# Attention and a feed-forward layer on one core: value tiles 144 instead of 132 bytes apart, attention outputs 288 instead of 264 bytes apart in PSUM

## The chip, the cores and the metric

One of the cores of a Trainium2 chip runs the whole program. The metric is the device time of one execution in microseconds, taken over several executions. The granted TensorE clock was 1.000 in all profiles shown below. Two words for the memories: SBUF holds what TensorE reads, PSUM the fp32 sums that it writes.

## The reference

Grouped-query attention (8 batches, 16 query heads, 4 key/value heads, 384 positions, head size 64), then a feed-forward layer with squared ReLU (1024 to 2048 to 1024), over 3072 tokens:

```python
scores = (1 / sqrt(64)) * q @ k.T          # k, v repeated for 4 query heads each
attn   = exp(scores - max) / sum
x      = (attn @ v) as [3072, 1024]
out    = (relu(x @ w_in) ** 2) @ w_out
```

## The kernel before

The kernel computes the scores transposed, so the exponentials can serve directly as the stationary operand (the one that is loaded first, by a weight load) of the second attention matmul. Its moving operand (the one that is streamed through, column by column) is a value tile of 128 positions by 64 values, with a column of ones behind them: output column 64 is then the softmax denominator. Each output needs three accumulating matmuls (j = 0, 1, 2), six outputs (f) share one PSUM bank, and VectorE divides them on the way out. A scheduler that runs on the host decides the order of all instructions from fixed costs, which do not depend on any address.

```python
DP = D + 2                                            # D = 64
v_aug = [sb(f"v_aug{i}", [128, NU, DP]) for i in range(2)]      # NU = 12 value tiles of a batch, bf16
...
R.add(eng, lambda e: e.tensor_copy(v_aug[b % 2][:, :, 0:D], v_st[b % NST][:, :, :]), ...)   # on GpSimd (POOL)
...
def av(b, c, banks):                                  # half a head group: 18 matmuls
    g, s2 = c // 2, c % 2
    i = pick(banks)
    po = bank(i)[:, 0:2 * NJ * DP].rearrange("p (f e) -> p f e", f=2 * NJ)      # fp32, PSUM

    def mm(pe, f0):
        for f in range(f0, f0 + NJ):                  # NJ = 3
            for j in range(NJ):
                w = expT[:, (b * NU + g * NJ + j) % NEX, f % 2, (f // 2) * 128:(f // 2) * 128 + 128]
                m = pe.matmul(po[:, f - 6 * s2, 0:D + 1], w, v_aug[b % 2][:, g * NJ + j, 0:D + 1],   # L383
                              start=(j == 0), stop=(j == NJ - 1))
        return m
    ...
    R.add("vector", lambda e: e.reciprocal(rinv[r].ap().unsqueeze(2), po[:, :, D:D + 1]), ...)
    ...
    srcv = po[:, :, 0:D].rearrange("p (s i) d -> p s i d", s=2)
    R.add("vector", lambda e: e.tensor_tensor(dst, srcv, rbv, ALU.mult), ...)
...
R.add("vector", lambda e, i=i: e.memset(v_aug[i][:, :, D:D + 1], 1.0), writes=[("v_one", i)])
# cuts: loads, transposes, scores (L358), exp (L368), up-projection (L440), down-projection (L496), scheduler
```

The softmax here doesn't subtract the row's maximum and nothing guards it: scores larger than these inputs give would overflow.

## Time and profile before

| | before |
|---|---|
| time, median of 3 runs | 427.7 us (427.55 to 427.76) |
| span of the profiled run | 426.2 us |
| TensorE busy | 420.4 us, 99% |
| matmuls of L383 | 1152, of 65 columns |

First the page of the kernel before: the span, the busy time of each engine, the chain of waits that ended last (share of the span by engine, then by line), and the groups that the change touches. A group's columns are line, engine, operation, output and inputs, shape and count; then busy us and mean ns of one; then idle time of the engine before it.

```profile
span 426.2 us, 7813 instructions
...
PE 420.4 (99%) x3435; PEld 232.0 (54%) x3464; DVE 157.9 (37%) x332; ACT 194.8 (46%) x194; POOL 55.4 (13%) x68
...
PE 96%; DMA 1%; issue 1%; ACT 1%; POOL 1%; DVE 0%; POOLq 0%
PE ps L440 40%; PE ps L496 39%; PE ps L383 8%; PE ps L358 7%; DMA q_st<-in_q_dram 1%; PE ps L337 1%; ACT expT L347 1%; PE ps L311 0%; PE ps L416 0%; POOL q_st L239 0%; PE ps L294 0%; POOL v_st L232 0%; DVE qT L318 0%; DVE y_sb L505 0%; POOL
...
L383 PEld LDWEIGHTS ps<-v_aug,expT 128*128 128x128 bf16 x1152 | 40.0, 97 | 6.9 <-issue 0.6
L383 PE MATMUL ps<-v_aug,expT 128*128 128x65 bf16 x1152 | 42.0, 193 | 0.0
L398 DVE TENSOR_TENSOR o_sb<-ps,rinv 128x384 bf16<-128x384 f32 x64 | 35.7, 558 | 2.2
...
L392 DVE RECIPROCAL rinv<-ps 128x6 f32<-128x6 f32 x64 | 12.2, 190 | 27.3 <-PE ps L383 27.3
```

TensorE is the bound: 96% of the chain, the feed-forward lines L440 and L496 taking four fifths of it, L383 8%. The 193 ns of one L383 matmul is a latency with much overlap; 42.0 us over 1152 matmuls is already only 36 ns each. The useful number is the time from one start to the next (a step; the expectations call a slow one a slip).

The chain in order of time (start us, us, what), two of its L383 runs with what follows each:

```profile
...
144.06 1.12 PE ps L383 x36
145.18 1.30 PE ps L440 x8
...
147.23 3.35 PE ps L440 x20
150.59 1.12 PE ps L383 x36
```

A full run of 36 matmuls takes 1.12 us, 31 ns per matmul, with no gap before or after it. And the view of line L383 (minimum, median and maximum duration in ns, then the start of the first and of the last in us):

```profile
...
L383 PE MATMUL ps<-v_aug,expT x1152: 191/193/205, 10.9 to 293.9; 128*128 128x65 bf16 x192
```

From the first L383 matmul to the last 283.0 us pass (10.9 to 293.9). Where the order of instructions is the same, this stretch compares kernels without their start-up, which differs between runs by some tenths of a us. It still contains every wait of TensorE on the way, so it is checked below against the steps themselves.

### The profile page before, as it was taken

To read this page: it belongs to the slowest core of one execution; us is meant where nothing else is said; L and a number is where in the kernel's file an instruction comes from. 1 tells how busy PE (TensorE), PEld (TensorE's weight loads), DVE (VectorE), ACT (ScalarE), POOL (GpSimd) and SP (SyncE) were. 2 spreads that over 40 slices of the span, in tenths; PEclk is the share of its full clock that TensorE was granted. 3 is DMA by queue.
4 is the path that set the end of the run, shared out by engine and by line. 5 is a ranking of instruction groups with operands and counts; after the bars stand their busy time and mean duration, and the time that the engine had idled before them with its cause. 6 is when DMAs were issued, how large, how long until landed. Compare 5 with 4: busy or idle time off the path is not lost.

```text
span 426.2 us, 7813 instructions
## 1 busy us (share of the span) xinstructions
PE 420.4 (99%) x3435; PEld 232.0 (54%) x3464; DVE 157.9 (37%) x332; ACT 194.8 (46%) x194; POOL 55.4 (13%) x68
## 2 busy tenths in 40 slices
PE   8999999999999999999999999999999999999997
PEld 6565554555545555455554455544564465446544
DVE  3664431343424443144442344422441244114412
ACT  6957730477355773547745377552240033003300
POOL 8680001234013004003100000000000000000000
DMA  9999999999789178938918321033001100110012
GB/s 177 184 184 200 186 201 226 180 158 158 145 182 167 26 106 125 149 94 134 120 45 180 92 34 25 12 88 102 25 2 49 74 26 2 49 74 26 1 67 82
DMA packets 96915, 44.30 MB, mean 104 GB/s; under 512 B 77296, under 2 KB 90864, under 8 KB 96880
## 3 DMA queue, kind: packets, MB, share of 16 engines
q0 software_dynamic: 36544, 17.44, 32.1%
q1 hardware_dynamic: 59664, 25.86, 28.7%
q8 instruction: 27, 0.44, 0.4%
q10 hardware_dynamic: 672, 0.49, 0.4%
q14 instruction: 8, 0.07, 0.1%
HBM read 35.65 MB, written 12.58 MB: 113 GB/s over the span
## 4 chain that ended last, share of the span: by engine, by line
PE 96%; DMA 1%; issue 1%; ACT 1%; POOL 1%; DVE 0%; POOLq 0%
PE ps L440 40%; PE ps L496 39%; PE ps L383 8%; PE ps L358 7%; DMA q_st<-in_q_dram 1%; PE ps L337 1%; ACT expT L347 1%; PE ps L311 0%; PE ps L416 0%; POOL q_st L239 0%; PE ps L294 0%; POOL v_st L232 0%; DVE qT L318 0%; DVE y_sb L505 0%; POOL ident L523 0%
## 5 line engine op out<-in xcount | busy, mean ns | idle before, releaser
L440 PE MATMUL ps<-xT,w_in_sb 128*128 128x384 bf16 x1024 | 174.8, 326 | 0.0
L496 PE MATMUL ps<-w_out_sb,h2T 128*128 128x512 bf16 (+2 forms) x755 | 167.5, 375 | 1.9 <-issue 0.5
L368 ACT ACTIVATE expT<-ps 128x3072 bf16<-128x3072 f32 x42 | 114.5, 2727 | 64.8 <-PE ps L358 64.0
L440 PEld LDWEIGHTS ps<-xT,w_in_sb 128*128 128x128 bf16 x1024 | 97.0, 98 | 69.6 <-issue 6.8
L450 ACT ACTIVATE h2T<-hr 128x384 bf16<-128x384 f32 x128 | 64.5, 520 | 140.9 <-DVE hr L448 140.9
L496 PEld LDWEIGHTS ps<-w_out_sb,h2T 128*128 128x128 bf16 x784 | 73.8, 98 | 87.1 <-issue 5.1
L448 DVE TENSOR_SCALAR hr<-ps 128x384 f32<-128x384 f32 x128 | 71.2, 557 | 106.4 <-PE ps L440 106.4
L505 DVE COPY y_sb<-ps 128x512 f32<-128x512 f32 (+2 forms) x49 | 33.4, 681 | 122.8 <-PE ps L496 122.8
L383 PEld LDWEIGHTS ps<-v_aug,expT 128*128 128x128 bf16 x1152 | 40.0, 97 | 6.9 <-issue 0.6
L383 PE MATMUL ps<-v_aug,expT 128*128 128x65 bf16 x1152 | 42.0, 193 | 0.0
L398 DVE TENSOR_TENSOR o_sb<-ps,rinv 128x384 bf16<-128x384 f32 x64 | 35.7, 558 | 2.2
L358 PE MATMUL ps<-qT,kT 64*128 64x512 bf16 (+1 forms) x336 | 34.6, 325 | 0.0
L358 PEld LDWEIGHTS ps<-qT,kT 64*128 64x128 bf16 x336 | 13.0, 94 | 20.7 <-issue 6.3
L392 DVE RECIPROCAL rinv<-ps 128x6 f32<-128x6 f32 x64 | 12.2, 190 | 27.3 <-PE ps L383 27.3
L271 POOL COPY v_aug<-v_st 128x768 bf16<-128x768 bf16 x8 | 6.6, 831 | 83.9 <-PE ps L383 68.4
L347 ACT ACTIVATE expT<-ps 128x1024 bf16<-128x1024 f32 (+1 forms) x20 | 16.9, 980 | 1.1 <-PE ps L337 0.8
L266 POOL COPY k_dup<-k_st 128x1536 bf16<-128x1536 bf16 x7 | 10.3, 1470 | 43.5 <-DMA k_st<-in_k_dram 43.5
L239 POOL DMA_DIRECT2D q_st<-in_q_dram x17 | 14.8, 883 | 0.9 <-POOLq L751 0.8
L207 POOL DMA_DIRECT2D k_st<-in_k_dram x7 | 5.3, 757 | 39.4 <-DMA qT<-q_st 39.4
L337 PE MATMUL ps<-qT,kT 64*128 64x384 bf16 (+2 forms) x48 | 7.5, 343 | 0.3 <-ACT expT L347 0.2
L249 POOL DMA_DIRECT2D w_in_sb<-in_moe_w_in_dram x8 | 7.1, 891 | 0.0
L232 POOL DMA_DIRECT2D v_st<-in_v_dram x8 | 6.3, 784 | 0.1
(26 smaller groups left out, 41.9 us busy)
## 6 DMA issues: line engine op xcount, KB each, us to landing
out_dram<-y_sb SPq DMA_DIRECT2D x47, 256.0 KB, 2.0
q_st<-in_q_dram POOLq DMA_DIRECT2D x14, 384.0 KB, 8.2
w_in_sb<-in_moe_w_in_dram POOLq DMA_DIRECT2D x8, 512.0 KB, 14.5
w_out_sb<-in_moe_w_out_dram POOLq DMA_DIRECT2D x4, 1024.0 KB, 30.8
v_st<-in_v_dram POOLq DMA_DIRECT2D x8, 192.0 KB, 9.8
k_st<-in_k_dram POOLq DMA_DIRECT2D x7, 192.0 KB, 4.4
q_st<-in_q_dram POOLq DMA_DIRECT2D x3, 192.0 KB, 5.4
xT<-o_sb SPq DMA_TRANSPOSE x28, 3.1
```

What stands on the lines that cost most here:

```text
L239: R.add("gpsimd", lambda g: g.dma_start(q_st[st][:, h0:h1, :], q[b, h0:h1].rearrange("h (p j) d -> p h (j d)", j=NJ)), writes=[("q_st", st ...
L347: R.add("scalar", lambda e: e.activation(dst, src, AF.Exp, scale=0.125), reads=keys, writes=[("expT", (b * NU + u) % NEX, t) for u, _, _ i ...
L358: m = pe.matmul(flat[:, k0 * HC + c0:k0 * HC + c1], kT[b % 2][64 * x:64 * x + 64, u + k0, :], q_cols(b, (u + k0) // NJ, x, c0, c1))
L368: R.add("scalar", lambda e: e.activation(dst, src, AF.Exp, scale=0.125), reads=keys, writes=[("expT", (n + m) % NEX, t) for m in range(2) ...
L383: m = pe.matmul(po[:, f - 6 * s2, 0:D + 1], w, v_aug[b % 2][:, g * NJ + j, 0:D + 1], start=(j == 0), stop=(j == NJ - 1))
L392: R.add("vector", lambda e: e.reciprocal(rinv[r].ap().unsqueeze(2), po[:, :, D:D + 1]), reads=[("bank", i)], writes=[("rinv", r)], cost=0.13)
L398: R.add("vector", lambda e: e.tensor_tensor(dst, srcv, rbv, ALU.mult), reads=[("bank", i), ("rinv", r)], writes=[("o_sb", o, s2)], cost=0.48)
L440: m = pe.matmul(bank(i)[:, 0:S], w_in_sb[:, kc, c * 128:(c + 1) * 128], xT[b % NXT][:, kc, :], start=(kc == 0), stop=(kc == NKC - 1))
L448: R.add("vector", lambda e: e.tensor_scalar_max(hr[r][:, :], bank(i)[:, 0:S], 0.0), reads=[("bank", i)], writes=[("hr", r)], cost=0.48)
L450: R.add("scalar", lambda e: e.activation(h2T[b % 2][:, c, :], hr[r][:, :], AF.Square), reads=[("hr", r)], writes=[("h2T", b % 2, c)], cost ...
L496: m = pe.matmul(bank(i)[:, 0:n], h2T[b % 2][:, c, i3 * 128:(i3 + 1) * 128], w_out_sb[:, c, c0:c1], start=(c == 0), stop=(c == NFC - 1))
L505: R.add("vector", lambda e: e.tensor_copy(ysl, bank(i)[:, 0:n]), reads=[("bank", i)], writes=[("y", yb)], cost=0.08 + n / 960)
```

## The change

The intent: 132 bytes is no multiple of 16, so the value tiles start at all four residues 0, 4, 8 and 12 modulo 16. At 144 = 9 x 16 bytes, all start on a multiple of 16. The PSUM outputs follow the same constant and go from 66 to 72 fp32 words apart.

```diff
-    DP = D + 2
+    DP, DV = D + 8, D + 8
...
-    v_aug = [sb(f"v_aug{i}", [128, NU, DP]) for i in range(2)]
+    v_aug = [sb(f"v_aug{i}", [128, NU, DV]) for i in range(2)]
```

## The prediction

> **What bounds the kernel.** TensorE. The page shows PE busy 99% of a 426.2 us span; the chain of waits that ended last is 96% PE, with clock 1.000. By line, that chain spends 40% on the up-projection (L440), 39% on the down-projection (L496), 8.3% on the attention-times-value matmuls (L383, the only ones the change touches) and 7% on scores.
>
> **What the change does.** Same instructions, same order, same shapes. Only addresses move: the 12 value tiles of one batch go from 132 to 144 bytes apart in SBUF (they are the moving operand, 65 bf16 columns read), and the six outputs of one PSUM bank from 264 to 288 bytes apart. Later SBUF buffers shift by 288 bytes, a multiple of 32.
>
> **Cost now.** L383 has 1152 matmuls; the chain shows a full run of 36 as 1.10 to 1.13 us. Taking start-to-start times of consecutive L383 matmuls from the trace (batches 1 to 7), the mean is 31.1 ns. Sorted by value tile n, so by start (132n mod 16):
>
> - start at 0 (n = 0, 4, 8): 29.2, 29.2, 29.2 ns, spread 0.4
> - start at 4 (n = 1, 5, 9): 33.1, 33.5, 29.2
> - start at 8 (n = 2, 6, 10): 32.2, 31.2, 32.9
> - start at 12 (n = 3, 7, 11): 29.5, 32.8, 31.9
>
> Tiles that start on a multiple of 16 bytes always run at 29.2; most others cost 2 to 4 ns more. The Trainium skill, "Advanced Engine Details and Errata", section Memory Cachelines, gives SBUF lines of 16 bytes; the trace agrees with a penalty of that period. The skill's "TensorE: Matmul & The Clock Gate", section "Wait — 56ns, not 53.3ns?", gives start-to-start of N / 2.4 GHz plus about 2.5 ns, 29.6 ns for N = 65: the aligned tiles are already there (29.2), so the floor is stream length.
>
> **Gain.** With 144 = 9 x 16 bytes every tile starts on a line. Estimate: (31.1 - 29.2) ns x 1152 = 2.2 us; batch 0 (31.8 ns) may give slightly more. All L383 blocks sit inside the unbroken PE chain, so nearly all of it should show.
>
> **PSUM half.** 264 and 288 are both multiples of 8, and the aligned tiles show 29.2 with spread 0.4 over all six output slots, so I give it nothing. The reciprocal (190 ns) and the normalizing multiply (557 ns) read runs of the same length and should not move.
>
> **Predicted time:** 425.5 us, 80% range 424.5 to 427.0. Faster by over 2%: 1%. Within 2%: 98%. Slower by over 2%: 1%.
>
> **What would show it.** L383 blocks of 36 fall from about 1.12 to about 1.05 to 1.06 us; start-to-start about 29.3 ns for every n, with no dependence on n; PE busy total down by about 2 us; L440 (163 ns apart), L496 (216 ns) and all DVE and ACT durations unchanged. If instead times still depend on n, the line theory is wrong; if all L383 get about 30.5, weight loads hold the rate and the gain is below 1 us.
>
> **What would make it wrong.** Weight loads (also 31 ns apart) may have their own limit that the slow tiles now hide. The saving could turn into waits for DVE, ACT or, in the first 60 us, weight DMAs. Shifted buffers (xT, w_in, w_out) might suffer from an address effect I cannot see, on 78% of the chain; a 1% change there would outweigh the gain.

## The result, and the profile after

| | before | after |
|---|---|---|
| time, median of 6 runs each | 427.87 us (427.55 to 428.86) | 427.52 us (427.21 to 428.14) |
| ratio, 95% interval | | 0.9991 (0.9977 to 1.0004) |
| span of the profiled run | 426.2 us | 425.4 us |
| TensorE busy | 420.4 us | 419.9 us |
| first to last L383 start | 283.0 us | 282.3 us |
| L383 start to start, mean | 31.13 ns | 30.45 ns |

A ratio is the mean time of one kernel's runs over that of the other's of the same rounds, so not quite the ratio of the medians quoted. Executions over 1.5% slower than the fastest of the same kernel are left out of the means. The median lies outside the predicted range (424.5 to 427.0): the gain is about a third of the 2.2 us forecast. The clock time alone cannot tell it from nothing, but the trace can.

The same parts of the page of the kernel after:

```profile
span 425.4 us, 7813 instructions
...
PE 419.9 (99%) x3435; PEld 231.6 (54%) x3464; DVE 157.8 (37%) x332; ACT 194.9 (46%) x194; POOL 55.3 (13%) x68
...
PE 96%; DMA 1%; issue 1%; ACT 1%; POOL 1%; DVE 0%; POOLq 0%
PE ps L440 40%; PE ps L496 39%; PE ps L383 8%; PE ps L358 7%; DMA q_st<-in_q_dram 1%; PE ps L337 1%; ACT expT L347 1%; PE ps L311 0%; PE ps L416 0%; PE ps L294 0%; POOL q_st L239 0%; POOL v_st L232 0%; DVE qT L318 0%; DVE y_sb L505 0%; POOL
...
L383 PEld LDWEIGHTS ps<-v_aug,expT 128*128 128x128 bf16 x1152 | 39.2, 97 | 6.9 <-issue 0.6
L383 PE MATMUL ps<-v_aug,expT 128*128 128x65 bf16 x1152 | 41.2, 193 | 0.0
L398 DVE TENSOR_TENSOR o_sb<-ps,rinv 128x384 bf16<-128x384 f32 x64 | 35.7, 557 | 2.2
...
L392 DVE RECIPROCAL rinv<-ps 128x6 f32<-128x6 f32 x64 | 12.2, 190 | 27.0 <-PE ps L383 27.0
```

Only L383 moved: 0.8 us less busy time, for its matmuls and for its weight loads (whose starts keep the same distance to those of the matmuls in both traces). VectorE's times are what they were. The order of instructions is the same on every engine. The chain in order of time and the view of L383, after:

```profile
...
143.70 1.09 PE ps L383 x36
144.79 1.30 PE ps L440 x8
...
146.85 3.36 PE ps L440 x20
150.21 1.09 PE ps L383 x36
```

```profile
...
L383 PE MATMUL ps<-v_aug,expT x1152: 191/193/204, 10.8 to 293.1; 128*128 128x65 bf16 x192
```

A run of 36 takes 1.09 us instead of 1.12; 1.05 to 1.06 was predicted. From the first L383 to the last it is 282.3 us (10.8 to 293.1), 0.7 less. Nothing took the gain back: in the list of waits, the scores (L358) wait for VectorE and for exp exactly as long as before:

```profile
...
PEld ps L358 <- DVE o_sb L398: 4.2, 13, 0.4
...
PEld ps L358 <- ACT expT L368: 2.0, 6, 0.4
```

```profile
...
PEld ps L358 <- DVE o_sb L398: 4.2, 13, 0.4
...
PEld ps L358 <- ACT expT L368: 2.0, 6, 0.4
```

The first fence is of before, the second of after; the columns are who waited for whom: us in total, times, longest us. Start to start, the up-projection runs at 162.8 ns in both traces and the down-projection (512 columns) at 216.0, leaving out ten double steps in each trace where a record is missing. So the missing 1.4 us was never gained at L383 itself.

Start-to-start times in ns of one run of 36 (batch 3, first key/value group), worked out from the start times in the two traces, show what happened:

```
before  29 35 32 30 32 33 29 33 33 29 32 33 29 32 32 29 34 32 29 33 32 29 34 32 29 34 32 29 33 32 30 32 32 29 33
after   29 35 30 29 29 35 29 29 29 35 30 29 29 29 35 29 29 30 29 35 29 29 29 29 35 30 29 29 35 29 29 29 30 35 29
```

The values of 32 to 34 that came with the mixed starts are gone, and the dependence on the tile n with them (batches 1 to 7, means for every n: 30.1 to 31.2). But every fourth or fifth step is now 35 ns, for tiles that all start on a multiple of 16 bytes (aligned, below), which the kernel before shows at 29.2 only. 29 ns is a step that happens, not a rate that lasts.

### The profile page after: what moved, and what is told of

Same layout as the page of the kernel before. It is cut to its first block, busy times and chain, and to the rows that moved or that the text cites. A ratio compares the mean times of both kernels' runs of the same rounds, so it can differ in the third digit from the quotient of the medians.

```text
span 425.4 us, 7813 instructions
## 1 busy us (share of the span) xinstructions
PE 419.9 (99%) x3435; PEld 231.6 (54%) x3464; DVE 157.8 (37%) x332; ACT 194.9 (46%) x194; POOL 55.3 (13%) x68
## 4 chain that ended last, share of the span: by engine, by line
PE 96%; DMA 1%; issue 1%; ACT 1%; POOL 1%; DVE 0%; POOLq 0%
PE ps L440 40%; PE ps L496 39%; PE ps L383 8%; PE ps L358 7%; DMA q_st<-in_q_dram 1%; PE ps L337 1%; ACT expT L347 1%; PE ps L311 0%; PE ps L416 0%; PE ps L294 0%; POOL q_st L239 0%; POOL v_st L232 0%; DVE qT L318 0%; DVE y_sb L505 0%; POOL ident L523 0%
## 5 line engine op out<-in xcount | busy, mean ns | idle before, releaser
L440 PE MATMUL ps<-xT,w_in_sb 128*128 128x384 bf16 x1024 | 174.8, 326 | 0.0
L496 PE MATMUL ps<-w_out_sb,h2T 128*128 128x512 bf16 (+2 forms) x755 | 167.5, 375 | 1.9 <-issue 0.5
L440 PEld LDWEIGHTS ps<-xT,w_in_sb 128*128 128x128 bf16 x1024 | 97.0, 98 | 69.5 <-issue 6.8
L496 PEld LDWEIGHTS ps<-w_out_sb,h2T 128*128 128x128 bf16 x784 | 73.8, 98 | 87.0 <-issue 5.1
L383 PEld LDWEIGHTS ps<-v_aug,expT 128*128 128x128 bf16 x1152 | 39.2, 97 | 6.9 <-issue 0.6
L383 PE MATMUL ps<-v_aug,expT 128*128 128x65 bf16 x1152 | 41.2, 193 | 0.0
L358 PE MATMUL ps<-qT,kT 64*128 64x512 bf16 (+1 forms) x336 | 34.6, 325 | 0.0
L358 PEld LDWEIGHTS ps<-qT,kT 64*128 64x128 bf16 x336 | 13.0, 94 | 20.7 <-issue 6.3
## 6 DMA issues: line engine op xcount, KB each, us to landing
w_out_sb<-in_moe_w_out_dram POOLq DMA_DIRECT2D x4, 1024.0 KB, 31.1
```

What stands on the lines that cost most here:

```text
L358: m = pe.matmul(flat[:, k0 * HC + c0:k0 * HC + c1], kT[b % 2][64 * x:64 * x + 64, u + k0, :], q_cols(b, (u + k0) // NJ, x, c0, c1))
L440: m = pe.matmul(bank(i)[:, 0:S], w_in_sb[:, kc, c * 128:(c + 1) * 128], xT[b % NXT][:, kc, :], start=(kc == 0), stop=(kc == NKC - 1))
L496: m = pe.matmul(bank(i)[:, 0:n], h2T[b % 2][:, c, i3 * 128:(i3 + 1) * 128], w_out_sb[:, c, c0:c1], start=(c == 0), stop=(c == NFC - 1))
```

## The experiments

All numbers called the mean are start to start between neighbouring L383 matmuls in batches 1 to 7, without the last of each run. Each comes from one trace; the pairs that differ only in the PSUM spacing (before and psum_only, after and sbuf_only) or in the element that is read (cols64 and bcast64) agree to 0.01 ns. The L383 records are complete (1152) in every trace; other lines lack a few, so totals of other lines are not compared. Edits are against the kernel after. "Wrong" means that the results do not match the reference and need not. The medians of the kernel before, in the rounds that were timed, lie between 427.9 and 428.0 us. The columns with numbers of bytes say where in a 16-byte line of SBUF the read starts, and how far apart the outputs lie in PSUM ("+ 4": each starts 4 bytes later).

| run | columns | start in a 16-byte line | PSUM | mean, ns | steps of 34 ns or more | checked result |
|---|---|---|---|---|---|---|
| before | 65 | 0, 4, 8, 12 mixed | 264 | 31.13 | 8% | right |
| after | 65 | 0 | 288 | 30.45 | 22% | right |
| sbuf_only | 65 | 0 | 264 | 30.46 | 22% | right |
| psum_only | 65 | mixed | 288 | 31.14 | 9% | right |
| cols64 | 64 | 0 | 288 | 29.14 | 0% | wrong |
| cols32 | 32 | 0 | 288 | 25.28 | 0% | wrong |
| cols66 | 66 | 0 | 288 | 30.44 | 22% | right |
| cols72 | 72 | 0 | 288 | 32.43 | 0% | right |
| ones_first | 65 | 14 | 288 + 28 | 30.88 | 34% | right |
| sbuf80 | 65 | 0 (160 apart) | 288 | 30.53 | 23% | right |
| sbuf68 | 65 | 0, 8 mixed | 288 | 30.64 | 17% | right |
| cols68 | 68 | 0 | 288 | 31.14 | 17% | right |
| cols64_132 | 64 | 0, 4, 8, 12 mixed | 264 | 29.98 | 5% | wrong |
| cols57 | 57 | 0 | 288 | 26.71 | 0% | wrong |
| bcast65 | 65 (one element repeated) | | 288 | 29.95 | 0% | wrong |
| bcast64 | 64 (one element repeated) | | 288 | 29.14 | 0% | wrong |
| cols64_psum4 | 64 | 0 | 288 + 4 | 29.96 | 0% | wrong |
| cols64_off8 | 64 | 8 | 288 | 29.21 | 0% | wrong |
| cols65_off8 | 65 | 8 | 288 | 30.02 | 9% | right |
| cols64_off4 | 64 | 4 | 288 | 29.21 | 3% | wrong |

### Which half of the change acts: sbuf_only and psum_only

```diff
-    DP, DV = D + 8, D + 8
+    DP, DV = D + 2, D + 8      # sbuf_only
+    DP, DV = D + 8, D + 2      # psum_only
```

> Value tiles 144 bytes apart, outputs still 264. Theory: the SBUF half does everything, so start-to-start of the L383 matmuls has the after kernel's pattern (29 ns with slips of 35 ns about every fifth, mean 30.4 to 30.5 ns in batches 1 to 7, no dependence on tile n) and the time is that of after (ratio to before 0.998 to 0.9995). Rival: the 35 ns slips come from outputs 288 bytes apart in PSUM; then they vanish here, mean 29.2 to 29.5 ns, about 1.4 us faster than after.

> Outputs 288 bytes apart, value tiles still 132. Theory: PSUM spacing is inert, so the mean is 31.1 ns and the start-to-start times depend on n as before (29.2 ns for n = 0, 4, 8), time as before within 0.2%. Rival: PSUM spacing causes slips; then aligned tiles n = 0, 4, 8 show 35 ns values here and the mean is above 31.5 ns, time up by half a us or more.

Measured: sbuf_only 427.48 us (median of 6), ratio 0.9996 (0.9980 to 1.0011; just above the forecast, with one of its six runs at a granted clock of 0.996 and 429.48 us), mean 30.46 ns. psum_only 427.76 us (median of 5), ratio 0.9998 (0.9986 to 1.0010), mean 31.14 ns with tiles 0, 4 and 8 at 29.2 to 29.4 as before. The views of line L383, first of sbuf_only, then of psum_only:

```profile
...
L383 PE MATMUL ps<-v_aug,expT x1152: 190/193/205, 11.5 to 293.8; 128*128 128x65 bf16 x192
```

```profile
...
L383 PE MATMUL ps<-v_aug,expT x1152: 190/193/206, 10.8 to 293.8; 128*128 128x65 bf16 x192
```

The stretch is 282.3 us (11.5 to 293.8), as in after, and 283.0 us (10.8 to 293.8), as in before. So the SBUF half is the whole effect, and the PSUM spacing does nothing. The clock times of sbuf_only could not have told this: 0.7 us is 0.2%, and its interval holds both that gain and none.

### Weight loads, or the 65th column: cols64 and cols32

My theory A was one of the prediction's own doubts: the weight loads cannot hold 29.2 ns. Theory B was that the 65th column costs more than its stream.

```diff
-    ... po[:, f - 6 * s2, 0:D + 1], w, v_aug[b % 2][:, g * NJ + j, 0:D + 1]
+    ... po[:, f - 6 * s2, 0:D], w, v_aug[b % 2][:, g * NJ + j, 0:D]              # cols64; 0:D // 2 in cols32
-    ... reciprocal(rinv[r].ap().unsqueeze(2), po[:, :, D:D + 1])
+    ... reciprocal(rinv[r].ap().unsqueeze(2), po[:, :, 0:1])
+    for i in range(6): ... memset(bank(i), 1.0)                                   # cols32 only
```

> After, but 64 value columns are read and written per matmul, without the column of ones (wrong result on purpose: no denominators). Weight loads unchanged. Theory A (the weight loads cannot follow at 29.2 ns for a whole run; their own limit is about 30.4 ns): mean stays 30.4 to 30.5 ns with 35 ns slips. Theory B (the 65th column costs the slip, since it starts a new 16-byte line): no slips, mean 29.0 to 29.3 ns, about 1.4 us faster than after.

> After, but 32 value columns per matmul (wrong result on purpose; six PSUM banks are filled at the start so that nothing unwritten is read, which shifts the schedule slightly). The stream is so short that only weight loads or instruction issue can set the pace. Theory A: mean 30.4 to 30.5 ns as in after. Theory B: mean well below 29 ns, or 29.2 ns without slips if 29.2 is the floor of the weight loads.

cols64: 425.91 us (median of 4), ratio 0.9952 (0.9938 to 0.9967), mean 29.14 ns, all steps but one 28 to 30. cols32: mean 25.28 ns, with the same weight loads. The views of L383, cols64 and then cols32:

```profile
...
L383 PE MATMUL ps<-v_aug,expT x1152: 192/193/204, 10.7 to 291.7; 128*128 128x64 bf16 x192
```

```profile
...
L383 PE MATMUL ps<-v_aug,expT x1152: 176/176/190, 11.9 to 288.8; 128*128 128x32 bf16 x192
```

With 64 columns the stretch is 281.0 us (10.7 to 291.7), 1.3 us less than after; cols32 has a slightly different order of instructions, so its stretch is not compared. Theory A falls: weight loads fit into 25.3 ns. One column costs 1.3 ns on average, where its stream is worth 0.4 (cols72 below: 3.3 ns for 8 columns). Of the 2.2 us predicted, that is about the 1.4 us that did not come: the floor I took from single steps belongs to 64 columns.

### How the cost grows with columns: cols66, cols68, cols72, cols57

```diff
-    ... po[:, f - 6 * s2, 0:D + 1], w, v_aug[b % 2][:, g * NJ + j, 0:D + 1]
+    ... 0:D + 2 / 0:D + 4 / 0:D + 8 on both                                       # the further columns are ones
-    ... memset(v_aug[i][:, :, D:D + 1], 1.0)
+    ... memset(v_aug[i][:, :, D:DV], 1.0)
# cols57: 0:D - 7 on both, reciprocal and memsets as in cols32
```

> After with 66 columns per matmul (the last one a second column of ones, result still right). Line theory (beginning a ninth 16-byte line costs about 8 columns' worth whether 1 or 2 of its elements are used): slips of 35 ns stay, mean 30.4 to 30.6 ns, no more than at 65 columns. Odd-count theory (65 is odd, and an odd column at the end costs extra): no slips, mean 29.9 to 30.1 ns, less than at 65 columns.

> After with 72 columns per matmul, nine full lines (result still right). From 64 columns at 29.2 ns, a plain stream of 2.4 columns per ns gives 29.2 + 8/2.4 = 32.5 ns. Line theory in its strong form (a ninth line costs as if all of it were read): mean near 30.5 ns as at 65 columns. If only the stream counts and the slips belong to 65 columns: 32.5 ns, no slips.

> After with 68 columns per matmul. Plain stream from 64 columns at 29.2 ns: 29.2 + 4/2.4 = 30.8 ns. If the unit of reading is a 16-byte line and its cost is hidden once the stream is long enough, 30.8 ns or slightly more, with few or no 35 ns slips. If any short last line costs about 3 extra columns on top of the stream, 31.8 to 32.1 ns with slips.

> After with 57 columns, seven full lines and one element of an eighth (wrong result on purpose). A plain stream gives 29.2 - 7/2.4 = 26.3 ns, which is above the 25.2 ns that 32 columns showed as the floor. Line theory: as 65 against 64, slips and a mean near 27.1 ns or more. Rival (something special to 65): 26.2 to 26.4 ns without slips.

The 2.4 columns per ns of these expectations agree with the trace: from the up-projection (384 columns, 162.8 ns) to the down-projection (512 columns, 216.0 ns), 128 columns take 53.2 ns.

cols66 costs what 65 does (30.44 ns, with the same 35 ns steps), which spoke for the line theory. cols72 runs at 32.43 ns without slow steps, so the strong form of that theory (all of a line's columns are paid) is refuted. cols68 shows 31.14 ns with slow steps of 36 to 37 ns: between the two forecasts. cols57 missed the line theory: 26.71 ns, no slow step, though its eighth line holds one element, while 26.3 was the plain stream. After these four I had a cost that depends on the column count, with no rule for it.

### Where the column is paid: bcast65, bcast64, cols64_psum4

```diff
# bcast65 (bcast64: D columns, as in cols64)
-    ... v_aug[b % 2][:, g * NJ + j, 0:D + 1]
+    ... v_aug[b % 2][:, g * NJ + j, 0:1].to_broadcast([128, D + 1])
# cols64_psum4 (on cols64)
-    ... po[:, f - 6 * s2, 0:D], w, ...
+    ... po[:, f - 6 * s2, 1:D + 1], w, ...                                        # and both reads of po by VectorE
```

> After, 65 columns written, but the moving operand repeats one value element 65 times (step 0, so a single SBUF line; wrong result on purpose). SBUF-line theory: no short ninth line, so no slips, and the mean is one column above the 64-column control: about 29.6 ns if that control reads 29.2. Rival (the column count itself, in the array or on the PSUM side, costs the slip): 30.4 to 30.6 ns with 35 ns slips.

> Control of the run before it: 64 columns from one repeated element (wrong result on purpose). Both theories: 29.1 to 29.3 ns without slips, as with 64 real columns, if reading with step 0 costs nothing by itself. If it costs something, only the difference between 65 and 64 counts: 0.4 ns under the line theory, 1.2 ns under the rival.

> 64 aligned columns, written 4 bytes later in PSUM, so that every output starts in the middle of 8 bytes (wrong result on purpose). SBUF-line theory: 29.1 to 29.3 ns, nothing changes. Rival (PSUM side): above 30 ns or slips.

65 columns from one repeated element run at 29.95 ns, nearly every step exactly 30; 64 at 29.14. The difference of 0.8 ns is neither forecast (0.4 or 1.2). cols64_psum4, the same 64 aligned columns written 4 bytes later, also runs at 29.96 ns, again nearly every step 30. That contradicts what I expected of the SBUF theory, and it names the second place: both kernels write across 33 pairs of fp32 words in PSUM, and 64 aligned columns write 32 pairs. An odd column and an odd start cost the same, one whole pair. Two columns' stream is 0.8 ns. The view of L383 in cols64_psum4:

```profile
...
L383 PE MATMUL ps<-v_aug,expT x1152: 193/195/204, 11.0 to 292.9; 128*128 128x64 bf16 x192
```

The stretch is 281.9 us (11.0 to 292.9), 0.9 more than the 281.0 of cols64.

The Trainium skill, "PSUM — Partial Sum Buffer", section Specifications (TRN2), gives PSUM lines of 8 bytes, two fp32 values. These runs agree with that unit (29.14 against 29.96 ns). The pair count also gives, as an estimate from cols64 at 0.82 ns per pair (two columns of 0.41 ns, from cols72 against cols64, so 72 fits by construction): 26.7 ns for 57 columns (measured 26.71), 30.0 for 66 (30.44), 30.8 for 68 (31.14). So 57 is explained by the PSUM side alone, and 65, 66 and 68 keep 0.3 to 0.5 ns that are not.

The first steps of a run in bcast65 are worth a look: 29, 29, then 30 to the end. A few steps can be faster than the lasting rate. That is the trap into which the prediction fell.

bcast64 is also a warning about the stretch: its steps are those of cols64 (29.14 ns), but its stretch is 282.1 us, 1.0 longer. The list of waits names the cause: at 68 us the down-projection waits for the weights w_out to arrive by DMA, the kind of wait that the prediction feared. It is there in cols66, sbuf80 and cols64_132 too, adding 0.4 to 1.0 us to their stretches; TensorE does not wait for w_out in before, after, psum_only, cols64, bcast65, cols64_psum4 or cols65_off8; in sbuf_only one weight load does, for 0.3 us, and no matmul. Why it comes in some traces was not tested, and each of these four is a single trace.

### Starts inside a line: ones_first, sbuf80, sbuf68, cols64_132

```diff
# ones_first: the ones at element 7, the values at 8 to 71, outputs likewise
+    ... po[:, f - 6 * s2, 7:D + 8], w, v_aug[b % 2][:, g * NJ + j, 7:D + 8]
# sbuf80 / sbuf68
+    DP, DV = D + 8, D + 16
+    DP, DV = D + 8, D + 4
# cols64_132 (on cols64)
+    DP, DV = D + 2, D + 2
```

> The column of ones moved in front of the values: the 65 columns start 14 bytes into a 16-byte line and end on a line's end (result right). Nine lines as in after, but the partly used one is the first. If the number of lines decides: mean 30.4 to 30.6 ns. If the short last line decides: 29.2 to 29.7 ns without slips, about 1 us faster than after. If the unaligned start decides, as for starts at 4, 8 and 12 in the kernel before: 31 to 33 ns.

> After with the value tiles 160 bytes apart, so that every one starts on a multiple of 32 bytes instead of 16. If 16-byte lines decide: as after, mean 30.4 to 30.6 ns with slips. If the unit were 32 bytes (after has every second tile at 16 modulo 32): slips vanish, mean near 29.5 ns.

> After with the value tiles 136 bytes apart: every start is a multiple of 8, every second one is 8 modulo 16. If the unit is 16 bytes: even n behaves as aligned, odd n costs as starts at 8 in the kernel before; mean 30.7 to 31.3 ns with dependence on n. If the unit is 8 bytes: no dependence on n, as after, mean 30.4 to 30.6 ns.

> 64 columns, but value tiles 132 and outputs 264 bytes apart as in the kernel before (wrong result on purpose, to compare with the 64-column kernel at 144 bytes: 29.2 ns, no slips). Line theory: tiles n = 0, 4, 8 touch 8 lines, all others 9, so the unaligned ones now pay what 65 columns pay; mean 30.3 to 31.3 ns, and the change is worth 1 to 2 ns per matmul here instead of 0.7. Rival (alignment matters only together with the 65th column): 29.2 ns for every n.

sbuf80: 30.53 ns, so a start at a multiple of 32 is no better than one at 16. sbuf68: 30.64 ns, just under its forecast. All even tiles run at 29.2, as expected, but of the odd ones only n = 1, 5, 7 and 11 run at 33.6 to 33.8; n = 3 and 9 start at 8 too and run at 29.1 to 29.2. So one step in three is slow in every group, whether one or two of its three tiles start at 8: the start of a tile does not set its own step (its clock was throttled in the first 20 us, 0.91; the mean leaves that batch out). ones_first: 427.89 us (median of 4), ratio 0.9988 (0.9967 to 1.0009), mean 30.88 ns, one step of 34 ns in every three: between two of its forecasts, and worse than after, so a short first line is no better than a short last one (its outputs also start 28 bytes in, so it is not a clean test, though they fill 33 pairs as those of after do). cols64_132: 427.28 us (median of 4), ratio 0.9987 (0.9970 to 1.0005), mean 29.98 ns, below its forecast, but 0.8 ns above cols64: alignment matters without the 65th column too.

### Constant starts: cols64_off8, cols64_off4 and cols65_off8

```diff
# values one half line, or one quarter line, further in (on cols64); cols65_off8 on after
-    ... tensor_copy(v_aug[b % 2][:, :, 0:D], v_st[b % NST][:, :, :])
+    ... tensor_copy(v_aug[b % 2][:, :, 4:D + 4], v_st[b % NST][:, :, :])          # off4: 2:D + 2
-    ... v_aug[b % 2][:, g * NJ + j, 0:D + 1]
+    ... v_aug[b % 2][:, g * NJ + j, 4:D + 5]                                      # cols65_off8: 65 columns
-    ... memset(v_aug[i][:, :, D:D + 1], 1.0)
+    ... memset(v_aug[i][:, :, D + 4:D + 5], 1.0)
```

> 64 columns, every tile starting 8 bytes into a 16-byte line, so nine lines are touched, the first and last half used (wrong result on purpose). SBUF-line theory: slower than the aligned 64 columns, 30.0 to 31.0 ns with slow steps, the same for every n. Rival: 29.2 ns.

> 64 columns, every tile starting 4 bytes into a 16-byte line (wrong result on purpose), outputs aligned in PSUM. If SBUF is read in units of 8 bytes, so that starts at 4 modulo 8 are what costs in the kernel before: 29.8 to 31.5 ns. If only the change from one alignment to another costs: 29.1 to 29.4 ns, as with a constant start at 8.

> 65 real columns (values, then ones; result right), every tile starting 8 bytes into a 16-byte line and ending 5 elements into the ninth line instead of 1. If the short tail of 1 or 2 elements makes the slips: mean 29.9 to 30.1 ns, the PSUM share alone, and about 0.5 us less than after. If a ninth line as such makes them: 30.4 to 30.6 ns. If an unaligned start costs at 65 columns: over 30.6 ns.

Both 64-column kernels run at 29.21 ns, 0.07 above the aligned one, although every tile starts inside a line and touches nine of them. So a start at 4 or 8, and with it a ninth line, costs next to nothing by itself at 64 columns. Starts of different alignment that follow each other do cost: mixed starts of 0, 4 and 8 alone (the first key/value group of cols64_132) give 29.77 ns, 0.6 more than each of the three kept constant (29.1 to 29.2). Constant starts at 12 were not run, so how much of the 0.8 ns of cols64_132 over cols64 is mixture is not known beyond that.

cols65_off8 is a right kernel, 426.91 us (median of 6), ratio 0.9975 (0.9954 to 0.9995), mean 30.02 ns. Its view of L383:

```profile
...
L383 PE MATMUL ps<-v_aug,expT x1152: 191/193/204, 10.9 to 292.8; 128*128 128x65 bf16 x192
```

The stretch is 281.9 us (10.9 to 292.8), 1.1 less than before and 0.4 less than after. With nine lines still, but five elements in the last instead of one, only the PSUM share is left over 64 columns (29.14 + 0.82 = 29.96). So the last 0.45 ns of after is a cost of how the 65 columns lie in the lines of SBUF, and goes when they start half a line later. That run changes two things, the start (0 to 8) and the tail (one element to five); that the short tail is what costs was the forecast that it met, but a start at 8 with a tail of one element was not run. It is the best right version found; it was not timed against after in the same rounds, so that it beats after rests on the traces: 30.02 against 30.45 ns.

## Why the prediction was right or wrong

- **What bounds it, and that the gain stays:** right. TensorE's chain is 96% in both, the waits of the scores are the same, L440, L496 and VectorE did not change. The 0.68 ns per matmul times 1152 is 0.78 us; the profiled spans differ by 0.8.
- **PSUM spacing worth nothing:** right (psum_only, 31.14 ns against 31.13). Both spacings are multiples of 8 bytes, and what costs is an output that does not fill its pairs (cols64_psum4).
- **No dependence on n after the change:** right in the main. The means by tile spread over 1.1 ns (30.1 to 31.2) where they spread over 4.3 before (29.2 to 33.5).
- **The step that failed: "Estimate: (31.1 - 29.2) ns x 1152 = 2.2 us", with "the aligned tiles are already there (29.2), so the floor is stream length".** The floor term was mis-sized: 30.45 ns was measured in place of 29.2 to 29.3. I had averaged single steps by tile and taken the fast class as a rate. Steps are not independent: after a slow one, the next run faster than what lasts. In cols65_off8 most steps (80%) are 29 or 30, 29.1 on average, under a lasting mean of 30.02; in cols64_off8 most (74%) are 28 or 29, 28.3 on average, under 29.21. The lasting rate of 65 columns is 29.14 (64 columns) plus 0.8 for the half-used 33rd pair of PSUM words (bcast65, cols64_psum4) plus 0.45 for the place of the read in its SBUF lines, probably its tail of one element (cols65_off8 against after).
- **The formula that seemed to confirm it:** the Trainium skill, "TensorE: Matmul & The Clock Gate", section "Wait — 56ns, not 53.3ns?", gives N / 2.4 GHz plus about 2.5 ns. That is 29.2 for 64 columns (measured 29.14) and 32.5 for 72 (32.43), but 29.6 for 65 (30.45 in after). An output that fills whole pairs is not enough for it: at 66 columns it gives 30.0 (measured 30.44).
- **Penalty of an unaligned start:** right that mixed starts cost, wrong in the reading. It is not the position in the 16-byte line as such: constant starts at 4 and 8 cost 0.07 ns at 64 columns. Their mixture costs (0.6 ns for starts of 0, 4 and 8 at 64 columns; the change, which also removes starts of 12, gained 0.7 at 65). A constant start at 14 did cost in ones_first (30.88 ns), so position is not shown to be free everywhere.
- **The doubt about weight loads:** the prediction said that "about 30.5" for all would mean weight loads hold the rate. The number came, the cause is refuted (25.28 ns in cols32).

Left open: how the read makes slow steps. A tail of one element costs nothing at 57 columns (26.71 ns, where the pairs alone give 26.7) and four elements cost 0.3 ns at 68; so "short tail" is a name for what 65 and 66 columns show, not a rule. That a mixture of starts costs, where each of 0, 4 and 8 alone does not, is shown but not explained.

## What to carry to other kernels

Take a floor from a kernel that sustains it, not from the fast steps of one that does not: in these traces fast steps follow slow ones, and a class of fast steps lies below the rate that lasts. For short matmuls, look at both ends: in this kernel an odd column count cost a whole pair of PSUM words, and read tiles that all start at 0, all at 4 or all at 8 in a 16-byte line cost less than tiles that start at changing places. An effect of 0.2% of the time was below what these timed runs resolve; the mean step of the affected line showed it clearly (31.13 against 30.45 ns, where two pairs of traces agree to 0.01 ns). The stretch from its first to its last start agrees with them only as long as no other wait falls into it, so look at the list of waits before comparing stretches.

## What the Trainium skill lacked or had wrong

- "TensorE: Matmul & The Clock Gate", section "Wait — 56ns, not 53.3ns?": N / 2.4 GHz plus about 2.5 ns holds for aligned tiles at 64 and 72 columns (29.14 and 32.43 ns) and not at 65, 66 or 68 (30.45, 30.44, 31.14) or, slightly, at 57 (26.71 against 26.25). The same section's floor of about 25 ns for short matmuls agrees with cols32 (25.28).
- "PSUM — Partial Sum Buffer", section Specifications (TRN2): it gives the 8-byte unit, but not that a contiguous output with an odd start pays for a whole further pair: 29.96 against 29.14 ns.
- "Advanced Engine Details and Errata", section Memory Cachelines: it gives SBUF lines of 16 bytes, a cost for changing lines at each access and the need of two hits on a line, without sizes, and nothing on starts. Here a constant start of the moving operand at 4 or 8 in the line cost 0.07 ns, and starts of 0, 4 and 8 that change from matmul to matmul 0.6 ns. No page has this.
- No page has that 65- or 66-column matmuls on aligned tiles, with one or two elements in a further SBUF line, run with steps of 35 ns (30.45 and 30.44 ns on average), and that 65 columns that start half a line later, with five elements in it, run with slow steps of 33 and 34 ns (30.02 on average). The two hits on a line that the section above asks for do not separate these: two elements cost as much as one.
